# Value loads of 128 rows, second means from rows of seven, and broadcasts on GpSimd, in a fused attention and MLP kernel

## Chip, cores, metric

The kernel runs on one core of a Trainium2 chip. Its metric is the device time of one execution in microseconds (us). The core has five engines with queues of their own: TensorE (PE in the profile; PEld are its weight loads), VectorE (DVE), ScalarE (ACT), GpSimd (POOL) and SyncE (SP), which issues all DMAs of this kernel. Each engine takes its instructions in order, and semaphores join the queues.

## What is computed

Attention with a local window and block means, then two MLPs, one after the other, in float32:

```python
# q, k, v: (2, 8, 768, 64); block 32, window 16, nb = 24 blocks
k_sum = k.reshape(B, H, nb, 32, D).max(axis=3)
v_sum = v.reshape(B, H, nb, 32, D).mean(axis=3)
scores_l = scale * q @ k.T, where |i - j| < 16, else -1e9
scores_s = scale * q @ k_sum.T + log(32)
a = softmax(concat([scores_l, scores_s]))        # 1e-9 added to the sum
x = a @ concat([v, v_sum])                        # to (1536, 512)
h = x @ w_in;  x = (h * tanh(softplus(h))) @ w_out        # 512 -> 2048 -> 512
x = ((x @ w1) * (x @ w2)) @ w3 @ w_out2           # 512 -> 1024 -> 1024 -> 512
```

The weights are 64-bit floats on arrival; the kernel turns each into two float32 parts, and every product of the MLPs is three matmuls (high by high, high by low, low by high).

## The kernel before

**Attention.** Heads go in four pairs `hp`, for two batches `b`. A set `s` is one pair, one batch and 256 query rows, 24 sets in all. The first eight sets (`early(s)`, batch 0, `j` 0 and 1) are the work of the beginning; the other sixteen run later, two at a time, between the products of the first MLP. A set goes: scores on TensorE (`score`, `score_two`), mask and maximum on VectorE (`peak`, line 984), exponentials on ScalarE (`expo`, 993), the row sums' reciprocal (`invert`: GpSimd 1001, VectorE 1003), `norm` on GpSimd (1007), a transpose on TensorE (`turn_p`) and its copy out (`store_p`, 1019), the product with the values (`attend`, `attend_two`), and its split into a high part on ScalarE and a low part on VectorE (`store_x`, 1069 and 1071).

A window of 64 query rows sees 96 key rows, and behind these stand the 24 block means, so that an operand has `KW` = 120 rows or columns. Values come in tiles of 96 rows; rows 96 to 119 are filled with the means on the chip.

**Early sets.** For each pair `list_means` and `list_keys` load the keys (`load_k`, 400 KB in 128 rows), the queries (`load_qp`, 256 KB in 128 rows), and the values in two pieces (`load_va` into columns `ROW` on of the tile `kvs[hp]`, 384 KB, and `load_vb`, 192 KB, both 96 rows). The maxima of the keys are a reduction on VectorE (`peak_k`, 885). The means of the values are matmuls (`parts_v`, `join_v`); `store_vm` (917 to 926) copies the result out of PSUM on VectorE, repeated eight times, into rows 96 to 119 of `kvs[hp]`.

**Later sets.** The values are loaded in pieces of 192 KB (`load_v`, 96 rows), the queries in pieces of 128 KB (`load_q`). For batch 1 `load_v8` loads the values once more, eight rows of 128 numbers in each of 96 partitions; `sum_v` (889) adds the eight on VectorE, reading them with a stride of 128, and a matmul with the band matrix `c32` makes the means (`mean_v`). `widen_v` (928) copies means into rows 96 to 119 of a value tile, on GpSimd. `widen_k` (932) builds the key tile `kw`: part 0, the windows, on GpSimd; part 1, the key maxima, on VectorE (941).

**Weights.** `list_weight` (247) loads 1 MB and decodes it: `shrink` on ScalarE or GpSimd, `low` (271), `sign` (277, not always), `join` (283) on VectorE, `hi` on ScalarE (290), `lo` on VectorE (295).

**Order.** Nothing runs in the order of the text. Each step is an `op(engine, cost, rank, reads, writes, function)`; `latest` walks backwards and finds how late each step may start, and `issue` then lists the steps engine by engine with these costs. The costs are so many us, in the code, and act on the order alone. While the first MLP has not begun, `issue` puts idle matmuls (`warm`) where it expects TensorE to wait. `list_turn`, `list_score`, `list_means` and `list_loads` make the steps of a set. `when` holds the rank of each set.

Of the kernel before, what the change touches and what calls it, by code (L numbers as in the profile page):

```python
# [17 lines left out]
P = 128  # L18
BLK = 32
# [15 lines left out]
AT2 = 7.8  # L35
YQ = {"B11": 48.7, "B21": 48.75, "T1": 48.8, "T3": 55.1, "B22": 57.1, "T2": 57.2, "T4": 59.1}
# [20 lines left out]
def fused_kernel(  # L57
# [189 lines left out]
    def list_weight(key, u, rank, due, seng, heng, leng):  # L247
# [58 lines left out]
        op(leng, 1.22 if leng == "dve" else 2.4, due, [d], [k], lo)  # L306
# [476 lines left out]
    c32 = cp.tile([96, NB], F32, name="c32")  # L783
# [5 lines left out]
    def constants():  # L789
# [43 lines left out]
        bands(c32, NB, 0, 4)  # L833
# [19 lines left out]
    def load_v8(b, hp):  # L853
        t = raw8[hp] = cp.tile([96, 8, P], F32, tag=f"v8{hp % 2}", name=f"v8{b}{hp}")
        nc.sync.dma_start(out=t, in_=v8_d[b, hp].rearrange("p (r d) -> p r d", r=8))

    def load_va(hp):

        nc.sync.dma_start(out=kvs[hp][0:96, ROW:], in_=vw_d[0, hp, :, 0:8 * P])

    def load_vb(hp):

        t = vbs[hp] = cp.tile([KW, 4, P], F32, tag=f"vw{hp}", name=f"vb{hp}", bufs=1)
        nc.sync.dma_start(out=t[0:96].rearrange("p g d -> p (g d)"), in_=vw_d[0, hp, :, 8 * P:12 * P])
# [10 lines left out]
    def load_v(s):  # L875
        b, hp, j = sets[s]
        t = st[s]["v"] = cp.tile([KW, 4, P], F32, tag=f"vw{s % RS}", name=f"vw{s}", bufs=1)
        nc.sync.dma_start(
            out=t[0:96].rearrange("p g d -> p (g d)"), in_=vw_d[b, hp, :, 512 * j:512 * (j + 1)]
        )  # L880
# [8 lines left out]
    def sum_v(b, hp):  # L889
        t = v8s[b, hp] = cp.tile([96, P], F32, tag=f"vs{hp % 2}", name=f"vs{b}{hp}", bufs=1)  # L890
        nc.vector.tensor_reduce(out=t, in_=raw8.pop(hp).rearrange("p r d -> p d r"), axis=AX.X, op=ALU.add)
# [24 lines left out]
    def store_vm(b, hp):  # L916

        src = banks[f"pm{b}{hp}"][96:KW, 0:P]
        if b:
            vm = vms[b, hp] = cp.tile([KW, P], F32, tag=f"vm{hp}", name=f"vm{b}{hp}", bufs=1)  # L920
            nc.scalar.copy(vm[96:KW], src)
        else:
            vms[b, hp] = kvs[hp][:, ROW:ROW + P]
            nc.vector.tensor_copy(
                kvs[hp][96:KW, ROW:].rearrange("p (g d) -> p g d", d=P), src.unsqueeze(1).broadcast_to([NB, 8, P])
            )
# [5 lines left out]
    def widen_k(s, part):  # L932

        b, hp, j = sets[s]
        if part == 0:
            kw = st[s]["k"] = cp.tile([P, 4, KW], F32, tag=f"kw{s % 2}", name=f"kw{s}", bufs=1)
            w = kts[b, hp][:, 256 * j:256 * j + 96]
            src = bass.AP(tensor=w.tensor, offset=w.offset, ap=[w.ap[0], [64, 4], [1, 96]])
            nc.gpsimd.tensor_copy(kw[:, :, 0:96], src)
        else:  # L940
            nc.vector.tensor_copy(
                st[s]["k"][:, :, 96:KW], kms[b, hp].unsqueeze(1).broadcast_to([P, 4, NB])
            )
# [89 lines left out]
    def attend_two(s, key):  # L1033
        xb = bank(key, f"x{s}")
        for w in range(2):
            x = st[s + w]
            for i in range(4):
                m, r = divmod(i, 2)
                for h in range(2):
                    hs = slice(64 * h, 64 * h + 64)  # L1040
                    nc.tensor.matmul(
                        xb[hs, 256 * w + 64 * i:256 * w + 64 * i + 64], lhsT=x["v"][:, i, hs],
                        rhs=x["pt"][:, 2 * h + m, 64 * r:64 * r + 64], start=True, stop=True,
                    )
# [43 lines left out]
    def list_means(b, hp, rank, ring):  # L1088
        key = ring.get()
        if b:  # L1090
            v8, vs = ("v8", hp % 2), ("vs", hp % 2)
            op("dma", 1.25, rank, [], [v8], load_v8, b, hp)
            op("dve", 1.15, rank, [v8], [vs], sum_v, b, hp)
            op("pe", 0.22, rank, [vs], [key], mean_v, b, hp, key)
        else:
            op("dma", 0.84, rank, [], [("qz", hp)], load_qp, hp)
            op("dma", 1.25, rank, [], [("va", hp)], load_va, hp)
            op("dma", 0.63, rank, [], [("vw", hp)], load_vb, hp)
# [4 lines left out]
        op("act" if b else "dve", 0.25 if b else 1.15, rank + 1.0 * (not b), [key], [("vm", b, hp)], store_vm, b, hp)  # L1103

    def list_loads(s, rank):
        op("dma", 0.5, rank, [], [("qz", s % RS)], load_q, s)
        op("dma", 0.63, rank + 0.01, [], [("vw", s % RS)], load_v, s)

    def list_score(s, rank, ring):
# [7 lines left out]
        for x in (s, s + 1):  # L1117
# [395 lines left out]
    when += [t + 1.7 * (s // 2) for t in (AT, AT2) for s in range(8)]  # L1513
# [165 lines left out]
def layout(q, k, v, w_in, w_out, w1, w2, w3, w_out2):  # L1679
# [11 lines left out]
    vw = np.stack([pad[:, :, 64 * g:64 * g + 96] for g in range(ng)], axis=3)  # L1691
# [31 lines left out]
```

## Time and profile before

| | |
|---|---|
| median of 3 runs | 563.01 us (563.0 to 563.5) |
| profiled execution: time | 565.25 us |
| profiled execution: span | 563.5 us |
| mean granted TensorE clock | 0.991 |
| TensorE busy | 549.3 us, 97% of the span |
| VectorE busy | 414.9 us, 74% |
| ScalarE busy | 296.4 us, 53% |
| GpSimd busy | 144.1 us, 26% |
| moved by DMA | 64.97 MB, mean 115 GB/s |

The span goes from the first to the last instruction of the profiled execution; its time holds what lies around that. Busy shares are means over the whole span; the stretches in the section on the rows tell more. Matmuls are pipelined, so that a busy TensorE may still run at the lower of its two clocks (1.2 and 2.4 GHz, written 0.50 and 1.00).

### The profile page before, as it was taken

To read this page: it belongs to the slowest core of one execution; us is meant where nothing else is said; L and a number is where in the kernel's file an instruction comes from. 1 tells how busy PE (TensorE), PEld (TensorE's weight loads), DVE (VectorE), ACT (ScalarE), POOL (GpSimd) and SP (SyncE) were. 2 spreads that over 40 slices of the span, in tenths; PEclk is the share of its full clock that TensorE was granted. 3 is DMA by queue.
4 is the path that set the end of the run, shared out by engine and by line. 5 is a ranking of instruction groups with operands and counts; after the bars stand their busy time and mean duration, and the time that the engine had idled before them with its cause. 6 is when DMAs were issued, how large, how long until landed. Compare 5 with 4: busy or idle time off the path is not lost.

```text
span 563.5 us, 8544 instructions
## 1 busy us (share of the span) xinstructions
PE 549.3 (97%) x3292; PEld 450.4 (80%) x3292; DVE 414.9 (74%) x674; ACT 296.4 (53%) x552; POOL 144.1 (26%) x176
## 2 busy tenths in 40 slices
PE   8797999999999999999999999999999999999997
PEld 8676777877788888888888888888888878788885
DVE  4599998333259997247698988988767687879892
ACT  4478889687625434326435445565344554434631
POOL 4256456333112210840421100000007352320000
PEclk9799999999999999999999999999999999999999
DMA  8995862210192000030126284322262242100003
GB/s 236 317 322 210 253 192 77 77 48 30 45 403 76 0 1 0 1 149 1 58 94 223 99 349 150 135 89 75 76 223 76 93 136 94 51 2 0 1 19 131
DMA packets 15848, 64.97 MB, mean 115 GB/s; under 512 B 1856, under 2 KB 3904, under 8 KB 10176
## 3 DMA queue, kind: packets, MB, share of 16 engines
q1 hardware_dynamic: 15808, 64.43, 33.1%
q8 instruction: 26, 0.43, 0.3%
q14 instruction: 14, 0.11, 0.1%
HBM read 61.28 MB, written 3.15 MB: 114 GB/s over the span
## 4 chain that ended last, share of the span: by engine, by line
PE 79%; DVE 8%; POOL 5%; DMA 3%; ACT 2%; issue 1%; SPq 0%; POOLq 0%; ACTq 0%; DVEq 0%
PE y L95 7%; PE y L97 7%; PE y L96 7%; PE h L95 5%; PE h L97 4%; PE h L96 4%; POOL dw12p L491 4%; PE wc L97 3%; PE wc L95 3%; PE wc L96 3%; PE s0g L519 2%; PE s0g L520 2%; PE s0g L521 2%; DMA qp<-in_q 2%; PE z L1427 2%; PE z L1426 2%
## 5 line engine op out<-in xcount | busy, mean ns | idle before, releaser
L491 POOL TENSOR_TENSOR dw12p<-dw12p 128x256 f32<-128x256 f32 x32 | 33.3, 1043 | 138.6 <-DVE w12p L295 136.7
L365 DVE TENSOR_TENSOR gl<-e,gh 128x512 fp32r<-128x512 f32 x32 | 26.7, 835 | 37.4 <-ACT gh L361 37.4
L95 PE MATMUL h<-xh,c 128*128 128x512 f32 x128 | 52.4, 409 | 0.0
L95 PE MATMUL y<-gh,c 128*128 128x512 f32 x128 | 51.4, 402 | 0.0
L97 PE MATMUL h<-xh,c 128*128 128x512 f32 x128 | 50.5, 394 | 0.0
L96 PE MATMUL h<-xl,c 128*128 128x512 f32 x128 | 50.4, 394 | 0.0
L97 PE MATMUL y<-gh,c 128*128 128x512 f32 x128 | 50.0, 390 | 0.0
L96 PE MATMUL y<-gl,c 128*128 128x512 f32 x128 | 49.9, 390 | 0.0
L993 ACT ACTIVATE sc<-sc,mx 128x120 f32<-128x120 f32 x96 | 36.6, 384 | 10.3 <-DVE mx L984 10.3
L357 ACT ACTIVATE e<-h 128x512 f32<-128x512 f32 x32 | 19.2, 599 | 27.7 <-PE h L97 27.3
L1007 POOL TENSOR_TENSOR sc<-sc,sm 128x480 f32<-128x480 f32 x24 | 27.3, 1139 | 17.3 <-DVE sm L1003 16.2
L95 PEld LDWEIGHTS h<-xh,c 128*128 128x128 f32 x128 | 24.4, 191 | 5.5 <-issue 0.5
L97 PEld LDWEIGHTS h<-xh,c 128*128 128x128 f32 x128 | 24.4, 190 | 5.4
L95 PEld LDWEIGHTS y<-gh,c 128*128 128x128 f32 x128 | 24.0, 188 | 5.4 <-issue 0.7
L96 PEld LDWEIGHTS h<-xl,c 128*128 128x128 f32 x128 | 24.5, 191 | 4.6
L97 PEld LDWEIGHTS y<-gh,c 128*128 128x128 f32 x128 | 24.0, 188 | 5.2
L290 ACT CAST w<-dw 128x1024 fp32r<-128x1024 f32 x20 | 21.1, 1054 | 12.9 <-DVE dw L283 12.8
L96 PEld LDWEIGHTS y<-gl,c 128*128 128x128 f32 x128 | 24.1, 188 | 4.5
L760 DVE TENSOR_TENSOR ya<-y,ya 128x512 f32<-128x512 f32 x32 | 21.8, 689 | 7.8 <-PE y L97 7.7
L290 ACT CAST c<-dc 128x1024 fp32r<-128x1024 f32 x16 | 16.9, 1054 | 17.1 <-DVE dc L283 16.8
L295 DVE TENSOR_TENSOR w<-dw,w 128x1024 fp32r<-128x1024 f32 x20 | 24.4, 1225 | 1.7 <-ACT w L290 1.6
L283 DVE SCALAR_TENSOR_TENSOR dw<-dw,w 128x1024 int32<-128x1024 int32 x20 | 25.0, 1256 | 0.5
(584 smaller groups left out, 1581.7 us busy)
## 6 DMA issues: line engine op xcount, KB each, us to landing
w<-in_w SPq DMA_DIRECT2D x20, 1024.0 KB, 4.8
c<-in_w SPq DMA_DIRECT2D x16, 1024.0 KB, 8.7
w12p<-in_w SPq DMA_DIRECT2D x8, 1024.0 KB, 4.8
kt<-in_kt SPq DMA_DIRECT2D x8, 400.0 KB, 4.2
vw<-in_vw SPq DMA_DIRECT2D x16, 192.0 KB, 3.8
qz<-in_q SPq DMA_DIRECT2D x16, 128.0 KB, 3.4
out<-c SPq DMA_DIRECT2D x8, 256.0 KB, 2.5
k<-in_kt SPq DMA_DIRECT2D x4, 400.0 KB, 8.7
```

What stands on the lines that cost most here:

```text
L95: nc.tensor.matmul(o, lhsT=lh, rhs=rh, start=start, stop=False)
L96: nc.tensor.matmul(o, lhsT=lh, rhs=rl, start=False, stop=False)
L97: nc.tensor.matmul(o, lhsT=ll, rhs=rh, start=False, stop=stop)
L283: nc.vector.scalar_tensor_tensor(out=a, in0=a, scalar=3, in1=words(T["raw"])[0], op0=ALU.logical_shift_left, op1=ALU.bitwise_or,)
L290: (nc.scalar.copy if heng == "act" else nc.vector.tensor_copy)(t[:, 0], T["a"])
L295: e.tensor_tensor(out=t[:, 1], in0=T["a"], in1=t[:, 0].bitcast(F32), op=ALU.subtract)
L357: nc.scalar.activation(T["e"], hb(), AF.Mish)
L365: nc.vector.tensor_tensor(out=T["gl"], in0=T["e"], in1=T["gh"].bitcast(F32), op=ALU.subtract)
L491: nc.gpsimd.tensor_tensor(out=quarter(o), in0=quarter(x), in1=quarter(y), op=sign)
L760: nc.vector.tensor_tensor(out=yacc[n][:, m], in0=banks[f"y{nm}_{m}"], in1=yacc[n][:, m], op=ALU.add)
L993: nc.scalar.activation(x["sc"][:, i, :], x["sc"][:, i, :], AF.Exp, bias=x["mx"][:, i:i + 1], scale=-1.0, accum_out=sm[:, i:i + 1],)
L1007: nc.gpsimd.tensor_tensor(out=sc, in0=sc, in1=sm.unsqueeze(2).broadcast_to([P, 4, KW]), op=ALU.mult)
```

## The change

Values come as 128 rows in place of 96, the last 32 of them zero in `vw`; the second copy `v8` becomes 5 groups of 7 numbers for each block and column, neighbours in memory, in 128 rows of which 120 count (a block of 32 is 7 + 7 + 7 + 7 + 4 and three zeros), and `c32` and the reduction follow that. The early means go out of PSUM once, on VectorE, into a tile `vm`, and GpSimd spreads them over the eight columns (`spread_v`). Part 1 of `widen_k` moves from VectorE to GpSimd. Costs of the planner change; `GAP` is a name for the 1.7 that stood there.

```diff
-        op("dma", 3.3, rank, [], [k], load)
+        op("dma", 2.8, rank, [], [k], load)
...
-        op("dve", 0.66, due, [], [k], low)
+        op("dve", 0.8, due, [], [k], low)
...
-        op(leng, 1.22 if leng == "dve" else 2.4, due, [d], [k], lo)
+        op(leng, 1.4 if leng == "dve" else 2.4, due, [d], [k], lo)
...
-    c32 = cp.tile([96, NB], F32, name="c32")
+    c32 = cp.tile([KW, NB], F32, name="c32")
...
-        bands(c32, NB, 0, 4)
+        bands(c32, NB, 0, 5)
...
-        t = raw8[hp] = cp.tile([96, 8, P], F32, tag=f"v8{hp % 2}", name=f"v8{b}{hp}")
-        nc.sync.dma_start(out=t, in_=v8_d[b, hp].rearrange("p (r d) -> p r d", r=8))
+        t = raw8[hp] = cp.tile([P, P, 7], F32, tag=f"v8{hp % 2}", name=f"v8{b}{hp}")
+        nc.sync.dma_start(out=t, in_=v8_d[b, hp].rearrange("p (d r) -> p d r", r=7))
...
-        nc.sync.dma_start(out=kvs[hp][0:96, ROW:], in_=vw_d[0, hp, :, 0:8 * P])
+        nc.sync.dma_start(out=kvs[hp][:, ROW:], in_=vw_d[0, hp, :, 0:8 * P])
...
-        t = vbs[hp] = cp.tile([KW, 4, P], F32, tag=f"vw{hp}", name=f"vb{hp}", bufs=1)
-        nc.sync.dma_start(out=t[0:96].rearrange("p g d -> p (g d)"), in_=vw_d[0, hp, :, 8 * P:12 * P])
+        t = vbs[hp] = cp.tile([P, 4, P], F32, tag=f"vw{hp}", name=f"vb{hp}", bufs=1)
+        nc.sync.dma_start(out=t.rearrange("p g d -> p (g d)"), in_=vw_d[0, hp, :, 8 * P:12 * P])
...
-        t = st[s]["v"] = cp.tile([KW, 4, P], F32, tag=f"vw{s % RS}", name=f"vw{s}", bufs=1)
+        t = st[s]["v"] = cp.tile([P, 4, P], F32, tag=f"vw{s % RS}", name=f"vw{s}", bufs=1)
...
-            out=t[0:96].rearrange("p g d -> p (g d)"), in_=vw_d[b, hp, :, 512 * j:512 * (j + 1)]
+            out=t.rearrange("p g d -> p (g d)"), in_=vw_d[b, hp, :, 512 * j:512 * (j + 1)]
...
-        t = v8s[b, hp] = cp.tile([96, P], F32, tag=f"vs{hp % 2}", name=f"vs{b}{hp}", bufs=1)
-        nc.vector.tensor_reduce(out=t, in_=raw8.pop(hp).rearrange("p r d -> p d r"), axis=AX.X, op=ALU.add)
+        t = v8s[b, hp] = cp.tile([KW, P], F32, tag=f"vs{hp % 2}", name=f"vs{b}{hp}", bufs=1)
+        nc.vector.tensor_reduce(out=t, in_=raw8.pop(hp)[0:KW], axis=AX.X, op=ALU.add)
...
-        if b:
-            vm = vms[b, hp] = cp.tile([KW, P], F32, tag=f"vm{hp}", name=f"vm{b}{hp}", bufs=1)
-            nc.scalar.copy(vm[96:KW], src)
-        else:
-            vms[b, hp] = kvs[hp][:, ROW:ROW + P]
-            nc.vector.tensor_copy(
-                kvs[hp][96:KW, ROW:].rearrange("p (g d) -> p g d", d=P), src.unsqueeze(1).broadcast_to([NB, 8, P])
-            )
+        vm = vms[b, hp] = cp.tile([KW, P], F32, tag=f"vm{hp}", name=f"vm{b}{hp}", bufs=1)
+        (nc.scalar.copy if b else nc.vector.tensor_copy)(vm[96:KW], src)
+
+    def spread_v(hp):
+        vm = vms[0, hp]
+        vms[0, hp] = kvs[hp][:, ROW:ROW + P]
+        nc.gpsimd.tensor_copy(
+            kvs[hp][96:KW, ROW:].rearrange("p (g d) -> p g d", d=P),
+            vm[96:KW].unsqueeze(1).broadcast_to([NB, 8, P]),
+        )
...
-            nc.vector.tensor_copy(
+            nc.gpsimd.tensor_copy(
                 st[s]["k"][:, :, 96:KW], kms[b, hp].unsqueeze(1).broadcast_to([P, 4, NB])
             )
...
-                        xb[hs, 256 * w + 64 * i:256 * w + 64 * i + 64], lhsT=x["v"][:, i, hs],
+                        xb[hs, 256 * w + 64 * i:256 * w + 64 * i + 64], lhsT=x["v"][0:KW, i, hs],
...
-        op("dma", 1.3, rank, [], [kt], load_k, key, b, hp)
+        op("dma", 1.1 if b else 1.15, rank, [], [kt], load_k, key, b, hp)
...
-            op("dve", 1.15, rank, [v8], [vs], sum_v, b, hp)
+            op("dve", 1.02, rank, [v8], [vs], sum_v, b, hp)
...
-            op("dma", 0.84, rank, [], [("qz", hp)], load_qp, hp)
-            op("dma", 1.25, rank, [], [("va", hp)], load_va, hp)
-            op("dma", 0.63, rank, [], [("vw", hp)], load_vb, hp)
+            op("dma", 0.75, rank, [], [("qz", hp)], load_qp, hp)
+            op("dma", 1.4, rank, [], [("va", hp)], load_va, hp)
+            op("dma", 0.72, rank, [], [("vw", hp)], load_vb, hp)
...
-        op("act" if b else "dve", 0.25 if b else 1.15, rank + 1.0 * (not b), [key], [("vm", b, hp)], store_vm, b, hp)
+        if b:
+            op("act", 0.25, rank, [key], [("vm", b, hp), ("vmt", hp)], store_vm, b, hp)
+        else:
+            op("dve", 0.25, rank + 1.0, [key], [("vmt", hp)], store_vm, b, hp)
+            op("pool", 1.4, rank + 1.0, [("vmt", hp), ("va", hp), held["k0", hp]], [("vm", b, hp)], spread_v, hp)
...
-        op("dma", 0.5, rank, [], [("qz", s % RS)], load_q, s)
-        op("dma", 0.63, rank + 0.01, [], [("vw", s % RS)], load_v, s)
+        op("dma", 0.35, rank, [], [("qz", s % RS)], load_q, s)
+        op("dma", 0.7, rank + 0.01, [], [("vw", s % RS)], load_v, s)
...
-            op("pool", 0.5, rank, [kt, *after], [kw], widen_k, x, 0)
-            op("dve", 0.25, rank, [("km", b, hp)], [kw], widen_k, x, 1)
-            op("pool", 0.86, rank, [("vm", b, hp)], [("vw", x % RS)], widen_v, x)
+            op("pool", 1.1, rank, [kt, *after], [kw], widen_k, x, 0)
+            op("pool", 0.35, rank, [("km", b, hp)], [kw], widen_k, x, 1)
+            op("pool", 1.0, rank, [("vm", b, hp)], [("vw", x % RS)], widen_v, x)
...
-        op("pool", 0.22, rank, [], [("sm", s % RS)], invert, s, 0)
+        op("pool", 0.34, rank, [], [("sm", s % RS)], invert, s, 0)
...
-        op("pool", 1.1, rank, [("sm", s % RS)], [sc], norm, s)
+        op("pool", 1.24, rank, [("sm", s % RS)], [sc], norm, s)
...
-    when += [t + 1.7 * (s // 2) for t in (AT, AT2) for s in range(8)]
+    when += [t + w * (s // 2) for t, w in ((AT, GAP), (AT2, 1.7)) for s in range(8)]
```

In the function that lays out the inputs, `vw` gets 32 zero rows behind its 96, and `v8` is laid out as five groups of seven for each block, columns outside, with eight zero rows behind the 120.

## Rows read from the trace of the kernel before

**Rows 1.** Stretches: start:end, length, each engine's busy us (instructions), PEclk, DMA share, GB/s.

```profile
24.00:45.55 21.55, 20.43 (x343) 17.05 (x335) 19.38 (x72) 16.23 (x53) 10.12 (x13) 0.98 1.01 345
45.55:82.40 36.85, 33.22 (x259) 25.59 (x257) 35.28 (x73) 31.73 (x77) 19.40 (x21) 0.95 0.63 206
...
56.00:58.00 2.00, 2.00 (x5) 1.61 (x6) 2.00 (x3) 1.97 (x4) 0.63 (x2) 0.50 0.27 51
...
82.40:558.00 475.60, 475.28 (x2407) 390.22 (x2405) 348.42 (x481) 239.43 (x387) 106.71 (x111) 1.00 0.25 91
```

**Rows 2.** TensorE's waits: for whom, us in total, times, longest.

```profile
PE s L953 <- DMA qp<-in_q: 4.0, 2, 3.2
PE s10h L968 <- DVE kw L941: 2.1, 1, 2.1
```

**Rows 3.** Chain that ended last, its first loads: start, us, from issue to landing.

```profile
2.17 6.25 DMA vb<-in_vw
8.44 10.35 DMA qp<-in_q
```

**Rows 4.** Timeline of SyncE: start and us of a DMA's issue.

```profile
13.58 0.35 SPq L868 DMA_DIRECT2D qp<-in_q  x1
...
90.45 0.33 SPq L878 DMA_DIRECT2D vw<-in_vw  x1
```

**Rows 5.** DMAs issued at 13.58, 90.45, 56.53, 106.52: size, us to landing.

```profile
qp<-in_q SPq DMA_DIRECT2D x1, 256.0 KB, 9.7
...
vw<-in_vw SPq DMA_DIRECT2D x1, 192.0 KB, 3.4
...
v<-in_v SPq DMA_DIRECT2D x1, 384.0 KB, 3.2
...
kt<-in_kt SPq DMA_DIRECT2D x1, 400.0 KB, 3.1
```

**Rows 6.** DMA totals of 2.25:3.75, 3.75:5, 8.75:17 and 24:32.

```profile
DMA packets 229, 0.55 MB, mean 364 GB/s; under 512 B 21, under 2 KB 21, under 8 KB 229
...
DMA packets 77, 0.22 MB, mean 175 GB/s; under 512 B 12, under 2 KB 12, under 8 KB 77
...
DMA packets 791, 2.00 MB, mean 243 GB/s; under 512 B 99, under 2 KB 99, under 8 KB 790
...
DMA packets 676, 3.28 MB, mean 411 GB/s; under 512 B 78, under 2 KB 295, under 8 KB 306
```

**Rows 7.** VectorE by groups, 24:45.5: out<-in xcount | busy, mean ns | idle before.

```profile
L924 DVE COPY k<-pm 24x1024 f32<-24x1024 f32 x2 | 2.5, 1230 | 0.8 <-PE pm L914 0.8
...
L1019 DVE COPY pT<-pt 120x512 f32<-120x512 f32 x3 | 2.0, 681 | 0.0
...
L941 DVE COPY kw<-km 128x96 f32<-128x96 f32 x2 | 0.8, 394 | 0.0
```

**Rows 8.** The same, 45.5:82.4.

```profile
L891 DVE TENSOR_REDUCE vs<-v 96x128 f32<-96x1024 f32 x4 | 7.8, 1972 | 0.0
...
L885 DVE TENSOR_REDUCE km<-kt 128x24 f32<-128x768 f32 x4 | 3.7, 935 | 0.0
...
L941 DVE COPY kw<-km 128x96 f32<-128x96 f32 x6 | 1.8, 324 | 0.0
```

**Rows 9.** Timeline of GpSimd: start, us, line, operation.

```profile
37.62 0.50 POOL L939 COPY kw<-k 128x384 f32<-128x384 f32 x1
...
39.02 1.50 POOL L939 COPY kw<-k 128x384 f32<-128x384 f32 x1
...
64.30 0.61 POOL L930 COPY vw<-k 24x512 f32<-24x512 f32 x1
...
92.95 1.59 POOL L930 COPY vw<-vm 24x512 f32<-24x512 f32 x1
```

**Rows 10.** Timeline of VectorE.

```profile
38.11 2.05 DVE L295 TENSOR_TENSOR c<-dc,c 128x1024 fp32r<-128x1024 f32 x1
...
60.60 1.21 DVE L295 TENSOR_TENSOR c<-dc,c 128x1024 fp32r<-128x1024 f32 x1
```

More of the change, by code (lines that the diff above doesn't have):

```diff
@@ L35 @@
 AT2 = 7.8
+GAP = 1.7
 YQ = {"B11": 48.7, "B21": 48.75, "T1": 48.8, "T3": 55.1, "B22": 57.1, "T2": 57.2, "T4": 59.1}
@@ L1583, in list_leave @@
         ks += [(x, i) for x in ("kt", "kw") for i in range(2)] + [("pt", i) for i in range(4)] + [(x, i) for x in ("v8", "vs") for i in range(2)]
-        ks += [(x, b, hp) for x in ("km", "vm") for b in range(B) for hp in range(HP)]
+        ks += [(x, b, hp) for x in ("km", "vm") for b in range(B) for hp in range(HP)] + [("vmt", hp) for hp in range(HP)]
         op("x", 0.0, 0, [], [*ks, *[("sl2", i) for i in range(NSL2)]], leave)
@@ L1690, in layout @@
     pad[:, :, WIN:WIN + S] = y
-    vw = np.stack([pad[:, :, 64 * g:64 * g + 96] for g in range(ng)], axis=3)
+    vw = np.zeros((B, HP, P, ng, P), v.dtype)
+    for g in range(ng):
+        vw[:, :, 0:96, g] = pad[:, :, 64 * g:64 * g + 96]
+    v8 = np.zeros((B, HP, NB, 5, 7, P), v.dtype)
+    z = y.reshape(B, HP, NB, BLK, P)
+    for i in range(5):
+        v8[:, :, :, i, :min(7, BLK - 7 * i)] = z[:, :, :, 7 * i:7 * i + 7]
+    v8 = np.concatenate([v8.reshape(B, HP, KW, 7, P), np.zeros((B, HP, P - KW, 7, P), v.dtype)], axis=2)
     a = w_in.reshape(KD, P, 16, P).transpose(2, 1, 0, 3).reshape(16, P, 512)
@@ L1699, in layout @@
         "kt": kt,
-        "vw": vw.reshape(B, HP, 96, ng * P),
+        "vw": vw.reshape(B, HP, P, ng * P),
         "q": np.ascontiguousarray(q.reshape(B, HP, 2, S, D).transpose(0, 1, 2, 4, 3)).reshape(B, HP, P, S),
-        "v8": y.reshape(B, HP, 96, 8 * P),
+        "v8": np.ascontiguousarray(v8.swapaxes(3, 4)).reshape(B, HP, P, 7 * P),
         "w": np.concatenate([g, c, d, e]).view(np.int64),
```

## The prediction

> **What bounds the kernel now.** I read the stretches first [rows 1]. From 82.40 to 558.00 us TensorE idles 0.32 us (475.60 - 475.28): what the change can win there is nothing, and what it can lose is open. So the 563.5 us are a ramp, then a solid block, and only the ramp is for sale. The main stream's first product starts at 45.55; between there and 82.40 TensorE idles 3.63 us (36.85 - 33.22), and the granted clock of 0.95 costs another 1.84 (0.05 x 36.85), most of it after one gap, when the clock stands at 0.50, its lower level, for 56.00:58.00. That is 5.5 us of loss. VectorE is busy 35.28 of those 36.85 us and 19.38 of the 21.55 before them: it sets the pace from 24 us on.
>
> Before 24 us it is the loads. TensorE's longest waits name them: 4.0 us for `qp`, and 2.1 us for the copy `kw` on VectorE [rows 2]. The chain gives the landings of the four early sets [rows 3]: the first set's last load is issued at 2.17 and lands at 8.42 (2.17 + 6.25); the third set's `qp` lands at 18.79. The fourth's `qp` is issued at 13.58 and lands 9.7 later, at 23.3 [rows 4, 5]. Three sets in 14.9 us are 4.95 us a set, of 1232 KB (400 + 256 + 384 + 192). The reader should see in the rates [rows 6] that a set is two kinds of transfer. While the first `kt` and `qp` (128 rows) move, the mean is 364 GB/s; when the first value rows (96 rows) follow, it is 175. In the mixture from 8.75 on it is 243, with weights of 128 rows 411. The packets of 2 to 4 KB in the first of these rows show that short rows alone don't make a transfer slow.
>
> **The change part by part.**
>
> *a. Value loads of 128 rows.* Removed: the 96-row shape. Added: a third more bytes (384 to 512 KB and 192 to 256 KB, so a set has 1424 KB). No row has a value load of 128 rows. The nearest is the 364 of `kt` and `qp`, of like row lengths: 1.458 MB / 364 GB/s = 4.0 us a set. Ends: the whole stretch runs at 411 (3.55 us a set), or at 243 as now (6.0 us; by rows in place of bytes, where 28 packets an engine become 32, 5.66). At 4.0 the first set lands some 0.95 earlier and the other three gain 0.95 each: the fourth lands 3.8 earlier, at 19.5. I take -3.7, since the work behind the fourth set is VectorE's and can move up with it. At 411 it would be -5.3; if the first set's start-up is as slow as now and only half of the rate is won, -1.9. Later loads of the change, 16 `vw` of +64 KB and 4 `v8` of +64 KB, are prefetches; if that cover were gone, one is 64 KB at 364 GB/s, 0.18 us.
>
> *b. The store of the early means.* VectorE copied the mean eight times over, 1230 ns [rows 7]; it will copy it once, 24x128 out of PSUM. From this row (1024 wide) and the 512-wide PSUM copy `pT` of 681 ns the slope is 1.07 ns an element, so 128 take 0.26 us: 0.97 saved. Two of the four lie after 24 us, where VectorE is the bound: -1.94. The other two lie before, beside waits for loads, and count nothing. The two `kw` copies that leave VectorE in that stretch give -0.79. Together -2.7.
>
> *c. VectorE between 45.55 and 82.40.* The reduction `vs` takes 1972 ns for 1024 elements read with a stride; the reduction `km` reads 768 neighbouring ones in 935 [rows 8]. With rows of seven side by side 896 elements come to 0.935 x 896/768 = 1.09 at most: 0.88 saved four times, 3.5 (0, if the short groups of seven cost as much as the stride). Six `kw` copies leave: 1.94. So 5.4 us of VectorE's time go, against 5.5 us that TensorE loses there. Part of that loss follows waits on GpSimd and ScalarE too, so I take half: -2.7 (ends 0 and -5.4).
>
> *d. What comes to GpSimd.* Its copy of 24x512 takes 0.61 and of 128x384 0.50 when nothing is in its way [rows 9]; at that slope a spread of 24x1024 is 1.05 us and a `kw` part of 128x96 some 0.25. They have a price elsewhere: the second copy of 128x384 took 1.50, and beside it VectorE's two-input L295 took 2.05, where alone it takes 1.21 [rows 9, 10]. So a collision costs VectorE between the length of the GpSimd instruction and 0.84. After 24 us and before 82.40 ten such instructions come, two spreads and eight `kw` parts. I let half of them collide at their own length, 1.05 + 4 x 0.25: +2.05 (ends 0, and 10 x 0.84 = 8.4). On GpSimd's queue stand the row sums and `norm` behind them, and `turn_p` on TensorE waits for `norm`. A store that goes VectorE, GpSimd, TensorE also has one hop more, but `attend` waits for the softmax of the same set anyway; if not, it is 1.05 + 0.26 against 1.23.
>
> The Trainium skill has a rule that speaks against this part ("SBUF — State Buffer", Who interferes with whom): VectorE with two SBUF inputs and GpSimd reading SBUF shut each other out for a whole instruction, and a `tensor_reduce` contends with nobody. The pair in rows 9 and 10 agrees with the first half. Read as a bare lock, all ten would cost their own lengths, 2 x 1.05 + 8 x 0.25 = 4.1, and the sum below would be -5.0, 558.0 us.
>
> *e. A new wait.* The load now writes the rows into which `widen_v` puts the means, so this copy has to wait for the load. At 92.95 it ran before its load had landed: issued at 90.45, 3.4 us, 93.85 [rows 4, 5, 9]. GpSimd would stand 0.9 us there, with `norm` and the next row sums queued behind it, and `turn_p` behind `norm`. That is in the solid block, where other products cover it; without the cover 0.9 us at each place where the copy comes first. I count 0. The matmul over 120 rows in place of 96, the bands of `c32`, and the constant `GAP` (1.7, as the literal was) cost nothing.
>
> *f. The order.* Several planner costs change, those of every weight's load and decode too, so the queues of VectorE and SP are laid out anew in the whole program. The block that idles 0.32 us can't gain from that. I count 0 and keep a rival for it.
>
> **Sum.** -3.7 - 2.7 - 2.7 + 2.05 = -7.05 us. The profiled execution took 565.25 us, its span 563.5; by the sum it becomes 558.2. The median of the runs shown, 563.01, lies 2.24 below that execution, which gives 556.0.
>
> **The rivals.**
>
> *R1: 128 rows take just as long as 96.* If one end of the path is loaded alike by both shapes, the zero rows travel free and nothing is won: a = 0, and 563.0 - 2.7 - 2.7 + 2.05 = 559.7. For it: alone, `v8` with 384 KB in 96 rows lands after 3.2 us, and `kt` with 400 KB in 128 rows after 3.1 [rows 5], though the latter was queued behind another load. Against: at 364 GB/s the 672 KB of `kt` and `qp` take 1.9 of the 4.95 us, so the value rows take 3.05 for 0.59 MB, 193 GB/s; the same time for 0.786 MB would be 258, which no full queue of 128-row loads shows. The Trainium skill gives this rule its form ("SBUF — State Buffer", Door 1: The DMA port swizzle): rows 0 to 63 reach one half of the ports and 64 to 127 the other, so by it 96 rows load the first half as 128 do. No row here splits the traffic by port.
>
> *R2: price per row.* The sets take 5.66 us, the fourth lands about 2.8 later, 2.4 of it passed on: 563.0 + 2.4 - 3.35 = 562.0. Against it stand the 364 and the 175, both of short rows.
>
> *R3: slower, by the collisions on GpSimd.* All ten collide at 0.84, score and attend wait for GpSimd as `s10h` waited for `kw`, so c yields nothing, and a gives its small end: -1.9 - 2.7 + 8.4 = +3.8, 566.8. It makes the kernel slower from seven collisions of ten on (-4.6 + 7 x 0.84 = +1.3). For it: VectorE's two-input instructions fill much of that stretch. Against: GpSimd idles for long times there, 19.40 busy of 36.85 [rows 1].
>
> *R4: slower, by the new order.* If four weights in the block come late by two instructions of 1.21 each, +9.7 - 7.05 = 565.7. Nothing in the trace speaks for it but that the block has no idle time to give.
>
> **How the numbers follow.** Forecast 0.63, R1 0.16, R2 0.07, R3 0.09, R4 0.05. The forecast's own range takes a from -5.3 to -1.9, c from -4.5 to -1.0 and d from 0.5 to 2.05: 551 to 559.5. R1 and R2 end inside a range drawn up to 562.3; R3 and R4 stay out with 0.14, and a little below 551. A measurement of this kernel can tell about 0.2%, 1.1 us, from no change: the forecast and R1 are faster (0.79), R2 is the same (0.07), R3 and R4 slower (0.14).
>
> **What would show it.** a: the fourth `qp` lands near 19.5 (23.3 by R1, 26 by R2), and the rate from 8.75 on is near 360. b: the store is 0.26 us, and the first product starts near 40. c: `vs` near 1.09 us. d: the spread near 1.05 us and two-input instructions of VectorE near 1.21 rather than 2. Idle time of TensorE before the block falls, and behind it none appears. The prediction is wrong if the value rows still move at 190 GB/s, or if the block from 82.40 on has gaps.

## The result

The changed kernel takes **557.52 us**, the median of 6 runs (557.47 to 559.06), against 563.64 for the kernel before (6 runs beside it, 563.0 to 565.07): ratio 0.9896, 95% interval 0.9881 to 0.9912. The prediction was 556.0 (551.0 to 562.3). The profiled execution took 557.47 us, its span is 555.8 at a granted clock of 0.996.

Single executions of one and the same program scatter with the clock that they are granted (before ran in 562.6 us at 0.999 and in 566.2 at 0.992), so the differences below come from ratios of many runs, and a difference under 2 us between two single traces says little.

Stretches of the changed kernel, with the columns of [rows 1]. The main stream's first product starts at 38.23 (before 45.55), so the stretches are cut there:

```profile
24.00:38.23 14.23, 12.17 (x225) 10.49 (x221) 12.12 (x28) 10.69 (x31) 10.04 (x12) 1.00 1.02 411
38.23:50.00 11.77, 8.61 (x41) 6.17 (x38) 11.54 (x28) 10.88 (x27) 9.36 (x11) 0.99 0.75 284
50.00:54.00 4.00, 4.00 (x39) 2.81 (x39) 2.98 (x15) 3.96 (x9) 1.01 (x2) 0.61 0.81 261
54.00:82.40 28.40, 28.40 (x240) 21.44 (x239) 25.98 (x63) 24.75 (x56) 16.52 (x22) 1.00 0.46 156
82.40:550.00 467.60, 467.50 (x2345) 384.61 (x2344) 340.31 (x451) 233.03 (x379) 102.32 (x113) 1.00 0.25 92
```

The first product came 7.32 us earlier and the span is 7.7 shorter. Behind that product little was won: TensorE idles 3.16 us in 38.23:50 (11.77 - 8.61) and the clock of 0.61 in 50:54 costs 1.56 more (0.39 x 4), 4.7 in all against the 5.5 that the prediction counted before. From 54 on the block is solid: 0.10 us of idle time in 82.40:550.

TensorE's waits in the changed kernel (for whom, us in total, times, longest), which answer to [rows 2]:

```profile
PE x L1031 <- DVE pT L1022: 2.1, 2, 1.0
PE pt L1017 <- POOL sc L1010: 1.8, 2, 1.5
PE h L96 <- ACT gh L362: 1.2, 1, 1.2
...
PE s L956 <- DMA qp<-in_q: 0.3, 1, 0.3
```

The 4.0 us for `qp` are 0.3, and the wait for `kw` is gone. In their place stand waits for `pT` on VectorE, in front of the first product, and for `norm` (1010) on GpSimd, behind it.

The loads, by the fourth `qp` (its issue on SyncE; its size and us to landing) and by the DMA totals of 3.75:5 and 8.75:17, as [rows 4 to 6]:

```profile
11.20 0.33 SPq L869 DMA_DIRECT2D qp<-in_q  x1
```

```profile
qp<-in_q SPq DMA_DIRECT2D x1, 256.0 KB, 7.7
...
DMA packets 147, 0.43 MB, mean 346 GB/s; under 512 B 15, under 2 KB 15, under 8 KB 147
...
DMA packets 1320, 3.40 MB, mean 412 GB/s; under 512 B 147, under 2 KB 147, under 8 KB 1314
```

It lands at 18.9 (before 23.3; forecast 19.5), and the rates are 346 for 175 and 412 for 243 GB/s. The first pair of rates tells little, since so short a stretch differs from order to order: with 128 rows 3.75:5 has 218 GB/s in e2, with 96 rows 257 in e1 (both below). The second pair tells more: 8.75:17 has 408 to 412 in all eight traces with value loads of 128 rows and 243 to 289 in the four with 96. The operations that the change touched, VectorE in 24:82.4 and GpSimd in 0:100 (columns of [rows 7]):

```profile
L284 DVE SCALAR_TENSOR_TENSOR dc<-dc,c 128x1024 int32<-128x1024 int32 x8 | 11.4, 1425 | 0.2
L296 DVE TENSOR_TENSOR c<-dc,c 128x1024 fp32r<-128x1024 f32 x7 | 9.0, 1286 | 0.2 <-ACT c L291 0.2
...
L892 DVE TENSOR_REDUCE vs<-v 120x128 f32<-120x896 f32 x4 | 4.2, 1074 | 0.0
...
L921 DVE COPY vm<-pm 24x128 f32<-24x128 f32 x1 | 0.3, 297 | 0.0
```

```profile
L944 POOL COPY kw<-km 128x96 f32<-128x96 f32 x12 | 6.3, 542 | 0.7 <-DVE km L886 0.5
L933 POOL COPY vw<-vm 24x512 f32<-24x512 f32 x7 | 6.2, 892 | 3.3 <-DMA vw<-in_vw 3.1
L926 POOL COPY k<-vm 24x1024 f32<-24x1024 f32 x4 | 4.2, 1038 | 8.4 <-DVE vm L921 5.9 <-issue 1.8 <-POOL sm L1004 0.5
```

The reduction takes 1.07 us (forecast 1.09), the store 0.30 (0.26), a spread 1.04 (1.05). These durations came in as forecast; the rate is above the 364 GB/s of the sum, and a `kw` part takes 0.54 in the mean in place of 0.25. The total is 1.5 us off. Whether these durations are what made the kernel faster is another question, and the experiments answer it differently.

### The profile page after: what moved, and what is told of

It reads as the page before. It is cut to its first block, busy times and chain, and to the rows that moved or that the text cites. A ratio compares the mean times of both kernels' runs of the same rounds, so it can differ in the third digit from the quotient of the medians.

```text
span 555.8 us, 8518 instructions
## 1 busy us (share of the span) xinstructions
PE 544.4 (98%) x3272; PEld 446.1 (80%) x3272; DVE 406.5 (73%) x658; ACT 296.3 (53%) x552; POOL 151.6 (27%) x196
## 4 chain that ended last, share of the span: by engine, by line
PE 90%; DVE 4%; DMA 2%; POOL 2%; ACT 1%; issue 1%; SPq 0%; DVEq 0%; POOLq 0%
PE y L96 8%; PE y L98 8%; PE y L97 8%; PE h L96 5%; PE h L98 5%; PE h L97 5%; PE wc L98 3%; PE wc L97 3%; PE s0g L520 3%; PE wc L96 3%; PE s0g L521 3%; PE s0g L522 3%; DMA qp<-in_q 2%; PE z L1434 2%; PE z L1433 2%; PE z L1435 2%
## 5 line engine op out<-in xcount | busy, mean ns | idle before, releaser
L492 POOL TENSOR_TENSOR dw12p<-dw12p 128x256 f32<-128x256 f32 x32 | 32.0, 999 | 146.2 <-DVE w12p L296 125.6
L296 DVE TENSOR_TENSOR w<-dw,w 128x1024 fp32r<-128x1024 f32 x20 | 24.3, 1220 | 2.8 <-ACT w L291 2.8
```

The costliest lines, as they stand in the source:

```text
L296: e.tensor_tensor(out=t[:, 1], in0=T["a"], in1=t[:, 0].bitcast(F32), op=ALU.subtract)
L492: nc.gpsimd.tensor_tensor(out=quarter(o), in0=quarter(x), in1=quarter(y), op=sign)
```

## The experiments

All times are medians; the difference is (ratio - 1) x 563.6, with its 95% interval, against the kernel before on the same chip. That kernel took 564.75 beside e1, e6 and e8, 563.27 beside e2 to e5 and 563.92 beside e9 to e11, on three chips, so the difference of two medians holds that of the chips; where the ratios give another, it stands beside it. "Order" says against which kernel the instructions stand in the same sequence on all five engines; "new" means that the planner laid them out anew.

| run | what differs | order | us | against before |
|---|---|---|---|---|
| changed kernel | | new | 557.52 | -5.9 (-6.7 to -5.0) |
| e1_rows96 | changed, window values in 96 rows again | changed | 558.42 | -5.7 (-7.4 to -3.9) |
| e10_strided_order | changed, strided reduction, cost 1.02 | changed | 558.18 | -5.9 (-7.0 to -4.7) |
| e4_sum_strided | the same, cost 1.95 | new | 564.6 | +0.7 (-0.8 to 2.3) |
| e2_kw_dve | changed, `kw` part 1 on VectorE | new | 557.58 | -6.5 (-8.1 to -4.9) |
| e3_store_dve | changed, store on VectorE, no spread | new | 554.61 | -9.5 (-11.2 to -7.8) |
| e5_old_costs | changed, costs of before | new | 556.84 | -7.2 (-8.7 to -5.5) |
| e11_store_costs | e3 with costs of before | new | 556.47 | -7.3 (-8.5 to -6.2) |
| e6_rows128 | before, value loads of 128 rows | before | 561.85 | -2.9 (-4.1 to -1.8) |
| e9_sum_alone | before, rows of seven | new | 560.45 | -3.7 (-5.0 to -2.4) |
| e8_costs_only | before, costs of the changed kernel | new | 563.96 | -0.3 (-1.4 to 0.7) |

### The loads: added alone, and taken back alone

e6_rows128, the kernel before with 128 rows for `va`, `vb` and `vw` only:

```diff
-        nc.sync.dma_start(out=kvs[hp][0:96, ROW:], in_=vw_d[0, hp, :, 0:8 * P])
+        nc.sync.dma_start(out=kvs[hp][:, ROW:], in_=vw_d[0, hp, :, 0:8 * P])
```

> The kernel before with its value loads (va, vb, vw) of 128 rows and nothing else changed; same order of the queues. Theory, loads: the landing of the fourth qp moves from 23.3 to about 19 us; with VectorE's work as before some of that is kept behind it: 559 to 560.5. R1: 563.3 to 564. If price goes by rows (R2): 565 or more.

e1_rows96, the changed kernel with 96 rows in the same three places (`v8` stays):

```diff
-        nc.sync.dma_start(out=kvs[hp][:, ROW:], in_=vw_d[0, hp, :, 0:8 * P])
+        nc.sync.dma_start(out=kvs[hp][0:96, ROW:], in_=vw_d[0, hp, 0:96, 0:8 * P])
```

> The changed kernel with only the row count of its value loads (va, vb, vw) put back to 96; order of the queues, reduction, stores and copies as changed. If the loads carry the larger part of the gain, as term a had it and more: the fourth qp lands near 23 us instead of 18.9, the first product starts near 43 instead of 38.2, and the time is 561 to 562.5. If 128 rows take as long as 96 (R1): 557.5, and the qp lands near 19 all the same.

Both keep the order of the kernel that they come from, so that only the transfers differ (e1 still reads an array padded to 128 rows, of which it takes 96). Added to the kernel before, the shape is worth 2.9 us, at 561.85 less of a gain than the theory had expected and more than R1's; taken from the changed kernel it costs nothing that the runs tell from zero (the interval of -5.7 holds -5.9). In e6 the rate in 8.75:17 is 410 GB/s and the fourth `qp` lands at 18.9 (11.83 + 7.1), as step a says. In e1 the rate falls to 289, but the landing moves by 1.2 us alone, to 20.1 (11.41 + 8.7), and not to the 23 that was expected. Its `qp` and the totals of 8.75:17:

```profile
qp<-in_q SPq DMA_DIRECT2D x1, 256.0 KB, 8.7
...
DMA packets 928, 2.38 MB, mean 289 GB/s; under 512 B 118, under 2 KB 118, under 8 KB 927
```

So 3.2 of the 4.4 us by which this landing moved in the changed kernel are there without the 128 rows. The order is a likely cause: e8 (below), with the loads and arrays of the kernel before in another order, moves 288 GB/s in 8.75:17 where that kernel moves 243. In e1 the first product comes 1.16 us later than in the changed kernel (39.39), and the medians differ by 0.9. In e6 the first product starts at 39.80, 5.75 us earlier, but TensorE, with the columns of [rows 1], idles 4.05 us in the 20 us from there and 1.57 in the next 40 (before 2.51 in its first 20):

```profile
39.80:59.80 20.00, 15.95 (x129) 12.03 (x128) 19.61 (x39) 16.93 (x47) 9.41 (x10) 1.00 0.60 203
59.80:100.00 40.20, 38.63 (x341) 29.66 (x339) 33.59 (x74) 34.11 (x70) 22.76 (x26) 1.00 0.50 163
```

The timeline of TensorE in e6 shows for whom (in brackets: idle before, and what ended it):

```profile
44.53 0.65 PE L1014 MATMUL pt<-ident,sc 128*120 128x128 f32 x4 [1.06 <-POOL sc L1007]
...
49.75 1.05 PE L968 MATMUL s10h<-kw,qz 64*64 64x120 f32 x32 [2.06 <-DVE kw L941]
...
55.34 0.79 PE L895 MATMUL pm<-vs,c 96*24 96x128 f32 x4 [0.91 <-DVE mx L984]
```

The wait of 2.06 us for `kw` is the one of [rows 2], moved up with everything else: VectorE is busy 19.61 of these 20 us, as it was before. The loss behind the first product is thus no smaller than before, but of another kind: up to 100 us e6 idles 5.62 us at full clock, where before idles 3.64 and its clock of 0.91 costs 1.8 more in the first 20.

### The reduction: its duration, and the order planned for it

e4_sum_strided takes the rows of seven out of the changed kernel (96 partitions, eight rows with a stride) and tells the planner 1.95; e10_strided_order is the same program but for that number, the last pair of lines:

```diff
-        nc.vector.tensor_reduce(out=t, in_=raw8.pop(hp)[0:KW], axis=AX.X, op=ALU.add)
+        nc.vector.tensor_reduce(out=t, in_=raw8.pop(hp).rearrange("p r d -> p d r"), axis=AX.X, op=ALU.add)
...
-            op("dve", 1.02, rank, [v8], [vs], sum_v, b, hp)
+            op("dve", 1.95, rank, [v8], [vs], sum_v, b, hp)
```

> The changed kernel with the second copy of the values in 96 partitions of eight rows and the reduction with a stride, as before (1.97 us each instead of 1.07). By term c two of the four lie before TensorE runs without gaps: 558.5 to 560. If VectorE isn't what TensorE waits for there: 557.5 to 558.

> The changed kernel with the reduction over eight strided rows in 96 partitions again, as in the run that lost the whole gain, but with the planner still told 1.02 for it, so that the instructions stand in the changed kernel's order and only the duration (1.07 to 1.97 us, four times) differs. Theory that the duration itself costs: 557.5 + 3.6 to 7 = 561 to 564.6, and TensorE waits for norm on GpSimd between the first product and 60 us. Theory that the 7 us came from the order laid out for a cost of 1.95: 557.5 to 559, with the first product near 38 to 40 and not at 45.

With the strided reduction in the changed kernel's order: 558.18, no difference to the changed kernel that the runs tell from zero. In the traces it is not for want of waits: in the 60 us from the first product on, TensorE idles 5.29 us in e10 and 3.16 in the changed kernel, but this execution of e10 keeps the full clock, where the changed kernel lost 1.56. With the order that 1.95 gives: 564.6, the whole gain gone, outside either of e4's expectations. The reduction lasts equally long in both (groups: min/median/max ns, first to last start; first e10, then e4):

```profile
L892 DVE TENSOR_REDUCE vs<-v x4: 1931/1952/2014, 48.0 to 62.2; 96x128 f32<-96x1024 f32 x4
```

```profile
L892 DVE TENSOR_REDUCE vs<-v x4: 1919/1954/1981, 51.3 to 62.0; 96x128 f32<-96x1024 f32 x4
```

And in e4 the first reduction starts at 51.3, after the first main product at 45.44, so that it can't have held that product up. What did is in TensorE's queue. First e10, in front of the first product `h`:

```profile
37.37 1.05 PE L971 MATMUL s8h<-kw,qz 64*64 64x120 f32 x32
38.35 0.50 PE L96 MATMUL h<-xh,c 128*128 128x512 f32 x1
```

Then e4, where three transposes and one product of the attention stand between `s8h` and `h`, with idle matmuls (`warm`) to fill the time:

```profile
33.33 1.20 PE L971 MATMUL s8h<-kw,qz 64*64 64x120 f32 x32
35.82 0.65 PE L1017 MATMUL pt<-ident,sc 128*120 128x128 f32 x4 [1.28 <-POOL sc L1010]
36.31 2.40 PE L788 MATMUL warm<-zero 128*128 128x128 f32 x20
39.45 0.69 PE L1031 MATMUL x<-pT,k 120*64 120x64 f32 x16 [0.75 <-DVE pT L1022]
40.07 2.50 PE L788 MATMUL warm<-zero 128*128 128x128 f32 x20
43.10 0.65 PE L1017 MATMUL pt<-ident,sc 128*120 128x128 f32 x4 [0.54 <-POOL sc L1010]
43.59 0.61 PE L788 MATMUL warm<-zero 128*128 128x128 f32 x4
45.03 0.65 PE L1017 MATMUL pt<-ident,sc 128*120 128x128 f32 x4 [0.83 <-POOL sc L1010]
45.44 0.48 PE L96 MATMUL h<-xh,c 128*128 128x512 f32 x1
```

`s8h` runs 4 us earlier than in e10, and yet `h` runs 7.1 later. So one number of the planner, on the same instructions, is worth 6.4 us (564.6 - 558.2; 6.6 by the ratios).

e9_sum_alone, the kernel before with rows of seven and a cost of 1.02 (1.15 before); the diff is the part on `v8`, `c32` and `sum_v` of the change, of which this is the core:

```diff
-        nc.vector.tensor_reduce(out=t, in_=raw8.pop(hp).rearrange("p r d -> p d r"), axis=AX.X, op=ALU.add)
+        nc.vector.tensor_reduce(out=t, in_=raw8.pop(hp)[0:KW], axis=AX.X, op=ALU.add)
...
-            op("dve", 1.15, rank, [v8], [vs], sum_v, b, hp)
+            op("dve", 1.02, rank, [v8], [vs], sum_v, b, hp)
```

> The kernel before, with nothing but the second means in rows of seven (the load of 128 rows, the reduction over neighbours, the matmul over 120 rows) and the planner's cost of that one reduction set to 1.02. VectorE loses 4 x 0.9 = 3.6 us between the first product and the block. If term c of the prediction has the right mechanism (half of VectorE's saving is passed on): 563.3 - 1.75 = 561.5, and the first product stays near 45.5, since all four reductions come after it. If the reduction carries the 7 us that went when it alone was taken back out of the changed kernel: 556 to 557. If it only matters once the loads are early (the early sets bound the ramp here, the reduction there): 562.5 to 563.5, no difference.

It is 3.7 us faster, and the first product comes neither earlier nor, as was expected, at 45.5, but 2.2 later, at 47.78 (in a profiled execution that was the slowest of seven). The gain lies behind it (20 us and up to 100 from there):

```profile
47.78:67.78 20.00, 19.66 (x147) 14.71 (x145) 20.00 (x39) 18.63 (x36) 11.64 (x12) 1.00 0.62 215
67.78:100.00 32.22, 32.22 (x280) 24.87 (x280) 24.65 (x65) 27.61 (x63) 19.54 (x20) 1.00 0.47 132
```

0.34 us idle at full clock, where before had 3.64 idle in its first 55 and a clock of 0.91 for 20 of them. This is the place and the kind of gain that step c names. But the order is new here too, and this run can't say which of the two did it.

### Order by the costs alone

e8_costs_only and e5_old_costs change nothing but the planner's numbers (before with those of the changed kernel, the changed kernel with the old ones), e.g.

```diff
-        op("dma", 3.3, rank, [], [k], load)
+        op("dma", 2.8, rank, [], [k], load)
...
-            op("pool", 0.5, rank, [kt, *after], [kw], widen_k, x, 0)
+            op("pool", 1.1, rank, [kt, *after], [kw], widen_k, x, 0)
```

> The kernel before with only the planner's costs changed (loads, decode, row sums, norm, widen), so only the order of the queues. If the order counts nothing, as step f had it: 563 to 564. If the order is where the gain over the sum came from: below 562. If the costs fit only the new transfers: above 564.

> The changed kernel planned with the costs of before for all steps whose work stayed. If the order counts nothing: 557 to 558. If the costs are part of the gain: 559 to 561.

-0.3 and, against the changed kernel, -0.7 (556.84 - 557.52; -1.3 by the ratios), neither told from zero: in these two places the set of numbers does nothing that the runs show. e8's first product starts at 50.81, 5.3 us later than before, with 0.74 us idle in the 60 us from there: the two trade against each other and the end stays.

### What went to GpSimd

e2_kw_dve gives part 1 of `widen_k` back to VectorE, e3_store_dve the early means (stored eight times over by VectorE, no spread):

```diff
-            nc.gpsimd.tensor_copy(
+            nc.vector.tensor_copy(
                 st[s]["k"][:, :, 96:KW], kms[b, hp].unsqueeze(1).broadcast_to([P, 4, NB])
...
-            op("dve", 0.25, rank + 1.0, [key], [("vmt", hp)], store_vm, b, hp)
-            op("pool", 1.4, rank + 1.0, [("vmt", hp), ("va", hp), held["k0", hp]], [("vm", b, hp)], spread_v, hp)
+            op("dve", 1.15, rank + 1.0, [key, ("va", hp), held["k0", hp]], [("vm", b, hp)], store_vm, b, hp)
```

> The changed kernel with part 1 of the key tile (128x96) back on VectorE, planned at 0.25 us. If moving it helped by its length on VectorE (terms b and c: 8 copies, 2.7 us, part of which counts): 558 to 559. If on GpSimd it costs as much as it saves (collisions: mean 0.47 us there instead of the 0.25 of term d): 557 to 558. If GpSimd's queue is what holds up TensorE between 43 and 49 us: 556 or less.

> The changed kernel with the early means stored by VectorE eight times over, as before, and no spread on GpSimd. By term b each of the stores on VectorE costs 0.93 us more, of which those behind the loads count: 558.5 to 559.5. If the stores lie beside waits for loads and exponentials: 557.5. If the spreads on GpSimd hold up norm: below 557.

`kw` makes no difference that the runs tell from zero (557.58; 0.6 faster by the ratios). The store does: **554.61 us, ratio 0.9831 (0.9801 to 0.9861)**, the fastest of all: without that part of the change, and in an order of its own, the kernel is 2.9 us faster (3.6 by the ratios). Its waits on TensorE in 24:82.4:

```profile
PE pt L1023 <- POOL sc L1016: 1.5, 3, 0.7
PE s12h L977 <- ACT vm L922: 0.5, 1, 0.5
PE s8h L977 <- POOL kw L950: 0.3, 1, 0.3
```

The 2.1 us for `pT` and the 1.2 for `gh` are gone. Yet its first product comes only 0.32 us earlier (37.91), so the gaps for `pT`, which lie in front of it, explain little of the gain. More lies behind: in the 60 us from there e3 idles 2.06 us, where the changed kernel idles 3.16, and it keeps the full clock, where the changed kernel lost 1.56:

```profile
37.91:57.91 20.00, 19.14 (x142) 14.31 (x141) 19.21 (x38) 17.77 (x42) 11.58 (x16) 1.00 0.88 326
57.91:97.91 40.00, 38.80 (x340) 29.89 (x339) 31.16 (x72) 33.09 (x71) 21.64 (x30) 1.00 0.35 103
```

The clock is no accident of one trace: the six executions of e3 were granted 0.999 to 1.000, those of the changed kernel 0.993 to 0.997.

In the changed kernel the first gap for `pT` comes in part out of a collision. VectorE, then GpSimd, around 30 us there:

```profile
29.99 1.82 DVE L284 SCALAR_TENSOR_TENSOR dc<-dc,c 128x1024 int32<-128x1024 int32 x1
31.73 0.68 DVE L1022 COPY pT<-pt 120x512 f32<-120x512 f32 x1
```

```profile
28.30 1.04 POOL L926 COPY k<-vm 24x1024 f32<-24x1024 f32 x1 [1.84 <-issue]
29.42 1.31 POOL L1010 TENSOR_TENSOR sc<-sc,sm 128x480 f32<-128x480 f32 x1
30.81 1.08 POOL L1004 TENSOR_SCALAR sm<-sm 128x4 f32<-128x4 f32 x1
```

`norm` stands behind the spread in GpSimd's queue and so falls on `dc`, which takes 1.82 us where 1.21 is its time alone; the operation on the row sums behind it (128x4) takes 1.08 where others take 0.22; `pT` is queued behind `dc`, whose 0.61 us too many are part of the 1.03 that TensorE stands at 32.47. The rule of the Trainium skill that the prediction weighed ("SBUF — State Buffer", Who interferes with whom) is the same thing, and both engines' rows agree with it. How much of the 2.9 us is the spread's and how much the new order's, e3 can't part.

e11_store_costs is e3 with the old costs:

> The changed kernel with the early means stored eight times over by VectorE as before (no spread on GpSimd) and the planner's costs of the kernel before, apart from the reduction's and the key means'. If both gains seen one by one add up: 557.5 - 3.0 - 0.7 = 553.8. If the costs do nothing by themselves: 554.6. If the order laid out by the old costs puts the store before the waits that the spread avoided: 556 to 557. TensorE's idle time in the 60 us from the first product on near 2 us in the first two cases (4.6 us of it with the spread was 3.2 us plus the clock's), over 3 in the third.

556.47: the time of the third expectation, though not its reason (0.20 and 0.06 us idle in the 60 us from the first product on, but that starts at 41.50, 3.6 later than in e3). Costs alone are worth 1.9 us here (2.2 by the ratios, with some 2 either way).

### Rows of a load, by themselves

Both kernels leave the whole computation out. e7_shapes loads in nine stages, eight loads each, and marks the end of each stage with a copy on VectorE; its output stores fell into the first four stages, so e12_shapes repeats the rows of 4 KB with the stores at the end.

```diff
+    def stage(rows, first):
+        for i in range(8):
+            nc.sync.dma_start(out=t[0:rows, i], in_=flat[first + i, 0:rows, 0:1024])
+        nc.vector.tensor_copy(flag[0:rows], t[0:rows, :, 0])
```

> Leaves the whole computation out and only loads: nine stages of eight DMAs each, each stage waiting for the one before. Stages: 128, 96, 64, 112 and 120 rows of 4 KB; 128 and 96 rows of 2 KB; 128 and 96 rows of 8 KB. If the row count sets the rate at any row length: 128 rows near 400 GB/s and 96 rows near 200 in all three pairs. If a load takes as long with 96 rows as with 128 (R1): 96 rows at three quarters of the rate of 128. If short rows are the cause: 2 KB slow, 8 KB fast, at either row count. 64, 112 and 120 rows tell whether the rate falls with the rows or jumps.

> Loads alone, with the whole computation left out: seven stages of eight loads of rows of 4 KB, with 128, 96, 64, 112, 120, 128 and 96 rows, one stage after the other and the outputs written only after the last. If the time of a load goes by its bytes: 128 rows 11.5 us (4.19 MB at 364 GB/s), 96 rows 8.6, 64 rows 5.8, 112 rows 10.1, 120 rows 10.8. If 96 rows take as long as 128 because one half of the path is loaded alike (rival R1): 11.5 for 96, 112, 120 and 128 rows and about 11 for 64. If shapes other than 128 rows are dealt out unevenly over the queue's engines, as the stage of 120 rows in the earlier run suggests (19.3 us): 96, 112 and 120 rows take longer than 128, 14 to 20 us, although they are fewer bytes.

The copies that end the stages of e12 (in brackets the time that VectorE waited, the length of a stage):

```profile
29.77 0.17 DVE L95 COPY flag<-t 96x8 int32<-96x8 int32 x1 [14.84 <-DMA t<-in_w]
42.85 0.17 DVE L95 COPY flag<-t 64x8 int32<-64x8 int32 x1 [12.91 <-DMA t<-in_w]
59.04 0.17 DVE L95 COPY flag<-t 112x8 int32<-112x8 int32 x1 [16.03 <-DMA t<-in_w]
73.99 0.17 DVE L95 COPY flag<-t 120x8 int32<-120x8 int32 x1 [14.78 <-DMA t<-in_w]
88.45 0.17 DVE L95 COPY flag<-t 128x8 int32<-128x8 int32 x1 [14.29 <-DMA t<-in_w]
102.72 0.17 DVE L95 COPY flag<-t 96x8 int32<-96x8 int32 x1 [14.10 <-DMA t<-in_w]
```

For rows of 4 KB, those of `va`, R1 holds: 96 rows take 14.1 and 14.8 us, 128 rows 14.3, though a quarter of the bytes is missing. The rule of the Trainium skill that gave R1 its form ("SBUF — State Buffer", Door 1: The DMA port swizzle) would have 64 rows last like 128; they take 12.9, nearly that. 112 rows take longer than 128 in both runs (16.0 here, 16.4 in e7), which neither R1 nor the bytes explain. e7 had 19.5 for 120 rows of 4 KB, where e12 has 14.8; why is open, since that stage came after the output stores, and uneven shares are not shown by it.

For rows of 2 KB, those of `vb` and `vw`, R1 doesn't hold: in e7, 128 and then 96 rows take

```profile
89.25 0.17 DVE L96 COPY flag<-t 128x8 int32<-128x8 int32 x1 [10.41 <-DMA t<-in_w]
97.52 0.17 DVE L96 COPY flag<-t 96x8 int32<-96x8 int32 x1 [8.10 <-DMA t<-in_w]
```

so that three quarters of the bytes take 0.78 of the time. At 8 KB it is 22.8 us for 128 rows and 27.7 for 96. Both sizes were run once.

## Why the prediction was right, and where its reasons were not

**a, the loads: right in the order of before, too large in the changed one.** Rate and landing came as forecast or better (412 GB/s, 18.9). R1, the same time for either shape, is true of loads of 4 KB rows by themselves (e12), not of 2 KB (e7), and false in the kernel's mixture, where it gives 281 GB/s (243 x 1424/1232) and the trace 410 (e6). Why the mixture gains more is open. The 175 GB/s that the prediction read as the rate of value rows is not a mark of the shape, as the other traces of that stretch show. By its own terms the end at 411 is 4 x 1.4 = 5.6 and not 5.3; no other number hangs on it but the lower end of the range. The worth, -3.7 with ends -5.3 and -1.9, holds in the order of before (-2.9) and not in the changed kernel's, where giving it back costs 0.2 us by the ratios and 0.9 by the medians, neither told from zero (e1): there 96 rows land only 1.2 us later, and not 3.8.

**b, the store: duration right, worth not borne out.** Forecast -2.7 with the `kw` copies, spread at +1.05 in step d. Undone, with an order of its own, the kernel is 2.9 us faster (e3) and not slower, and how much of that is the order's isn't known, so the sign of the store's own worth stays open. What the trace shows against the step: 0.97 us less on VectorE is not 0.97 less on the path when GpSimd, with `norm` queued behind the spread, comes up instead. The `kw` copies, in an order of their own too, make no difference that the runs tell from zero (e2).

**c, the reduction: the place right, the size not settled.** In the kernel before, with an order of its own, rows of seven bring 3.7 us behind the first product (e9), inside the ends 0 and -5.4. In the changed kernel's order, giving back the 3.5 us of VectorE lengthens TensorE's idle time in the traces (5.29 for 3.16), but not the time of the kernel (e10). In the traces, the loss behind the first product is 4.7 us after and 5.5 before, so what c was to remove stayed for the most part.

**d, collisions: durations right but for the `kw` part, the price on VectorE too high.** The spread is 1.04; a `kw` part takes 0.26 alone, and 0.54 in the mean of twelve, since some collide (1.50 for two, 1.93 for two). VectorE's two-input instructions `dc` (1.425 in the mean of eight) and L296 (1.286 of seven) take 2.25 us more in 24:82.4 than at 1.21 each; before, the same sum over L283 (1.252 of seven) and L295 (1.482 of six) is 1.93. So VectorE lost 0.3 us more and not 2.05, and its means are nowhere near R3's 2.05 an instruction. R3 didn't come.

**e, the new wait: there, and covered.** GpSimd stood 3.1 us for the load in three places, 1.25 at 61.42 the longest; TensorE idles nothing in 54:82.40, where two of them lie, and 0.10 us in 82.40:550, where the third does.

**f, the order: this is the step that failed.** It was counted at 0, since the block "can't gain from that", with R4 at 0.05 for a loss in the block. But the order decides the ramp: 6.4 us by one cost on the same instructions (e4, e10), 1.9 by a set of costs (e3, e11), and nothing told from zero by the like set elsewhere (e8, e5). R4's mechanism is real, its place is the ramp and not the block, and its sign is not fixed. In the changed kernel the shape of the loads and the duration of the reduction can each be given back alone at no cost that the runs tell from zero, so its 5.9 us can't be read as the sum of -3.7, -2.7, -2.7 and +2.05, near as that comes. Giving both back at once in that order was not tried; that the rest is the order is argued from e1 (where the landing stays early with 96 rows), e4 and e10, not shown.

So the number was right in part by luck: a sum of parts each costed against the order of before, while the planner laid out another. What held is the bound read from [rows 1]: only the ramp was for sale, and the block stayed solid.

## What to carry to other kernels

Where a planner lays out the queues, a change of durations is two changes: run the new durations in the old order and the new order with the old durations, and believe a part's worth only where both agree. An earlier landing moves the first product, but what then waits is the engine that was busy all along; look at the idle time and the clock behind the first product and not only at where it starts. Before moving a copy to an idle engine, look at what is queued behind it there: GpSimd had the time, and still `norm`, behind the spread, ran into `dc`.

## What the runs showed of the hardware

- Eight loads by themselves take, at rows of 4 KB, 14.1 to 14.8 us for 96 rows, 16.0 for 112, 14.8 for 120, 14.3 for 128 and 12.9 for 64 (e12). At 2 KB it is 8.1 for 96 and 10.4 for 128, at 8 KB 27.7 and 22.8 (e7). So 32 more rows cost nothing at 4 KB and something at 2 KB.
- Among other loads 96 rows move 243 GB/s in one order and 288 in another (8.75:17, before and e8), 128 rows 408 to 412 in each of eight traces.
- GpSimd's operation on 128x4 numbers, 0.22 us by itself, took 1.08 beside VectorE's two-input `dc`, which took 1.82 in place of 1.21. It lost 0.86 us so; `norm`, 0.99 by itself, lost 0.88 at 42.18 (1.87) beside another `dc`: the collision was as dear for a tiny operation as for a large one.
- The early low clock is gone with the early waits for loads: 0:24 ran at 0.88 before and at 1.00 after. TensorE then fell to 0.61 for 50:54 just behind its three gaps of 0.37, 1.46 and 1.18 us. e10 has the like gaps (4.11 us of idle time in 20) and stayed at 1.00, so that the gaps alone don't decide it; four other executions of e10 were granted 0.996 or 0.997, as the changed kernel was.
